# Three unused tiles of 32 bytes that shift where matmul operands start in SBUF

## The chip, the cores and the metric

The kernel runs on one core of one Trainium2 chip, as one launch. The metric is the time of the device in microseconds. Before the change it is 565.58 us, the median of three runs (565.38 to 565.63).

## The reference

Three layers follow each other, all in float32. The first is attention over hash buckets: two batches of 8 heads, 768 positions, 64 dimensions. The second is a feed-forward layer over the 1536 resulting rows of 512, with a softmax gate and a normalisation between its two products. The third sends each row to one of 8 experts of two products each.

```python
def _attn_ref(q, k, v, proj):
    q_bucket, k_bucket = ...                      # signs of q @ proj and k @ proj, as 6 bits
    scores = scale * np.matmul(q, k.transpose(0, 1, 3, 2))
    scores = np.where(q_bucket == k_bucket, scores, -1e9)
    attn = softmax(scores)
    return np.matmul(attn, v)

def _moe_ref(x, w_in, w_out, g_ln):               # 1536 x 512 -> 1024 -> 512
    h = x @ w_in
    solu = h * softmax(h)
    ln = (solu - mean(solu)) / np.sqrt(var(solu) + 1e-06) * g_ln
    return ln @ w_out

def _moe2_ref(x, w_gate, w_output_gate, w1, w2):  # 8 experts, 512 -> 1024 -> 512
    e_idx = np.argmax(x @ w_gate, axis=1)
    for e in range(8):
        mask = e_idx == e
        h = np.maximum(x[mask] @ w1[e], 0.0)
        out[mask] = gate_w[mask, None] * eom[mask, e, None] * (h @ w2[e])
```

## The kernel before

The order of every engine's work is written out by hand in the program; no scheduler moves anything. There are three stages.

**Attention** (class `Attention`, to about 207 us). The scores (line 243) are matmuls of 384 columns in pairs: the two heads of a pair lie on partitions 0 to 63 and 64 to 127, and each takes one half of TensorE's rows. Their operands are tiles `Hq`, `Lq`, `Fq`, `Hk`, `Lk`, `Fk` of type fp32r. The products with the values (line 294) and the sums (line 314) have plain float32 operands. During the first microseconds bf16 matmuls on a tile of zeros (`fill`, line 195) run, which compute nothing that is used; small bf16 products (`bits` with `tab`, line 228) make the bucket masks.

**Feed-forward** (class `Ffn`, about 211 to 367 us). For each of 12 blocks of 128 rows the first product (method `up`, line 634, tiles `h<-wi,xh` and `h<-wi,xl` in the profile) is two halves of 12 matmuls of 512 columns, and the second (method `down`, line 634, `y<-wo,lh` and `y<-wo,ll`, for some blocks `h<-wo,...`) is 24 matmuls of 512 columns. Each float32 operand is split into a high and a low part of type fp32r (`xh`, `xl`; `wi0`, `wi1`; `lh`, `ll`; `wo0`, `wo1`), and three of the four part products are added up in PSUM. In the profile's names the first tile behind the arrow is the moving operand, the second the stationary one (transposes the same: `t<-ident,e` moves the identity over the block `e`). Every matmul has a weight load of its own (PEld).

**Experts** (class `Experts`, about 375 to 559 us). Each of the 8 experts has 96 matmuls of 256 columns (line 1163: the rows `xh`, `xl` move, for expert 0 `e`; the weights `wh`, `wl` are stationary) and 48 of 512 columns (line 1185: the weights move, the halves of the hidden layer are stationary, which are kept in the tiles `wo0` and `wo1`, no longer needed as weights by then). Weights come by DMA into four staging tiles `ws` and are split into `wh` by ScalarE (line 1071) and `wl` by GpSimd and VectorE (line 1073) ahead of their use.

**Where the tiles lie.** A tile has one start address, the same in every partition. Tiles come from pools that lie one behind the other, from the left end of the SBUF or (with `side="right"`) from its right end; within a pool, tiles follow each other at multiples of 32 bytes. The first address and its remainder by 64, as the program is built before the change:

| tiles | start | remainder by 64 |
|---|---|---|
| attention: `Hk`, `Lk`, `Hq`, `Lq`, `Fk`, `Fq` | 81792 and on, every 3072 | 0 |
| attention: `pt0` to `pt7` in turn | 145024 and on, every 3104 | 0, 32, 0, 32, ... |
| zeros of the bf16 matmuls: `fill` | 52640 | 32 |
| `wi0`, `wi1` | 196576, 212960 | 32 |
| `wo0`, `wo1` | 19872, 36256 | 32 |
| feed-forward `xh`, `xl`, `lh`, `ll` | 97760 to 118240 | 32 |
| experts' `wh` and `wl` | 163808 and on, every 8192 | 32 |
| experts' `xh`, `xl`; `e`; `ws` | 116384; 85408; 52640 | 32 |
| `ident`, `ones`, `projw`, `wg32` | 17472, 17216, 17088, 16576 | 0 |

Inside a tile, the pieces that one matmul reads lie at multiples of 512 bytes, but for the query slices of the attention, which start 0, 4 or 8 bytes in.

Of the kernel before, what the change touches and what calls it, by code (L numbers as in the profile page):

```python
# [8 lines left out]
F32 = mybir.dt.float32  # L9
# [7 lines left out]
P = 128  # L17
# [1219 lines left out]
def counts(tc, C, cnt):  # L1237
    nc, ci = tc.nc, C["ci"]
    nc.vector.tensor_tensor(out=cnt, in0=cnt, in1=C["first"], op=ALU.subtract)
    nc.vector.tensor_reduce(out=C["gap"], in_=cnt, axis=AX.X, op=ALU.max)  # L1240
    nc.vector.tensor_copy(ci[:, 0:E], cnt)
    nc.vector.tensor_copy(ci[:, E:E + 1], C["gap"])
# [54 lines left out]
@with_exitstack  # L1297
def tile_kernel(
    ctx: ExitStack, tc, q, k, v, proj, moe_w_in, moe_w_out, moe_g_ln, moe2_w_gate, moe2_w_output_gate, moe2_w1, moe2_w2, out
):  # L1300
    nc = tc.nc
    cp = ctx.enter_context(tc.tile_pool(name="cp", bufs=1))
    scratch = tc.dram_tile([SLOTS + N, ROW], F32, name="scratch")
    cnt = cp.tile([P, E], F32, name="cnt")

    def clear(z, n):
        nc.sync.dma_start(
            out=scratch[4 * P * n:4 * P * (n + 1), :].rearrange("(p a) r -> p (a r)", p=P).rearrange("p (b x) -> p b x", b=10),
            in_=z.unsqueeze(1).to_broadcast([P, 10, 2 * ROW // 5]),
        )  # L1310

    def blank(z):
        nc.gpsimd.memset(z, 0.0)
        for n in range(3):
            nc.sync.dma_start(
                out=out[4 * P * n:4 * P * (n + 1), :].rearrange("(p a) r -> p a r", p=P),
                in_=z.unsqueeze(1).to_broadcast([P, 4, DM]),
            )

    with tc.manual_schedule(), ExitStack() as c0, ExitStack() as c4:  # L1320
        c1 = c0.enter_context(ExitStack())
        xp = c1.enter_context(tc.tile_pool(name="xT", bufs=1, side="right"))
        xT = xp.tile([P, 2, 4, S], F32, name="xT")
        keep = c4.enter_context(tc.tile_pool(name="wo", bufs=1))
        W = Weights(tc, cp, xp, keep, moe_w_in, moe_w_out, moe_g_ln, moe2_w_gate, moe2_w_output_gate)
        with ExitStack() as c2:
            cv = c2.enter_context(tc.tile_pool(name="cv", bufs=1))
            at = Attention(tc, c2, q, k, v, xT)
            at.load(0, "qk")
            at.C = C = {}  # L1330
            at.open(c2)
            make_consts(tc, cp, cv, proj, C)
            at.preset()
            nc.gpsimd.tensor_copy(cnt, C["first"])
            nc.gpsimd.memset(W.wg, 0.0)
            at.warm(10)
            at.tables()
            at.warm(1)
            z = cv.tile([P, 2 * ROW // 5], F32, name="zero")
            nc.gpsimd.memset(z, 0.0)  # L1340
            extra = W.steps(cv, at.bank)
            at.run(8, extra, [lambda n=n: clear(z, n) for n in range(7)])
        stg = c4.enter_context(tc.tile_pool(name="ws", bufs=4, reuse_waits="tile"))
        ep = c4.enter_context(tc.tile_pool(name="ep", bufs=2, reuse_waits="tile"))
        r0 = c4.enter_context(tc.tile_pool(name="r0", bufs=1, reuse_waits="tile"))
        ex = Experts(tc, C, stg, moe2_w1, moe2_w2, scratch, out, r0, W.wo)
        with ExitStack() as c2:
            ffn = Ffn(tc, c2, C, xT, W, scratch, cnt, ep, ex)
            for u in range(4):
                ex.fetch(u)  # L1350

            def ahead():
                c1.close()
                return ex.ahead(c0)

            ffn.run(ahead, blank)
        with ExitStack() as c2:
            ex.open(c2)
            ex.run(lambda: counts(tc, C, cnt))
    overflow(tc, C, moe2_w1, moe2_w2, scratch, out, ex.done)  # L1360
# [36 lines left out]
```

## Time and profile before

| what | us |
|---|---|
| median of three runs | 565.58 |
| the profiled execution, its own time | 566.14 |
| its span, first to last instruction | 564.4 |
| attention, to the last score matmul | about 207 |
| feed-forward products | 211 to 367 |
| experts' products | 375.5 to 558.5 |

The profiled execution lies 0.56 us above the median, and 1.7 us of its time lie outside the span. Engines are PE (TensorE's matmuls), PEld (its weight loads, which run beside matmuls), DVE (VectorE), ACT (ScalarE) and POOL (GpSimd). The duration of a matmul in the trace includes its way through the array, and matmuls overlap; how fast they follow each other is read from their starts. A row of the timeline merges equal instructions that follow each other on an engine, gives the start of the first, the time to the end of the last, and their number.

### The profile page before, as it was taken

The numbers are of one execution on the slowest core, as the hardware profiler recorded it, in microseconds if no ns is written. First come the engines' busy times: TensorE is split into PE (matmuls) and PEld (weight loads), VectorE is DVE, ScalarE is ACT, GpSimd is POOL, SyncE is SP. The second block draws the span as 40 slices with busy tenths as digits, with TensorE's granted clock in tenths as the row PEclk, the third lists the DMA queues.
The fourth block names the chain that finished last, engine by engine and source line by source line (L and its number), as shares of the span: only waits on it lengthen the run. The fifth ranks groups of instructions, "written<-read, shape, count | busy, mean of one in ns | idle before, by whom it ended". The sixth has DMA issues, their size and how long they took to land. (4 is left out here: it accounts for less than half of the span.)

```text
span 564.4 us, 9890 instructions
## 1 busy us (share of the span) xinstructions
PE 551.3 (98%) x3826; PEld 438.2 (78%) x3826; DVE 393.2 (70%) x793; ACT 266.1 (47%) x450; POOL 330.3 (59%) x270
## 2 busy tenths in 40 slices
PE   8899999999999999999999999999999999999995
PEld 3776667776667747888888887889989989899894
DVE  7978888888978657767687777665674664646631
ACT  3457657575675641332224232337355462564530
POOL 5399898898989883001001040327875956958741
PEclk9899999999999999999999999999999999999999
DMA  3545646455452445500000040329829376597201
GB/s 112 163 139 149 156 147 180 136 150 149 153 141 94 116 133 202 216 0 1 1 1 0 1 95 0 113 73 351 293 81 334 101 285 219 177 339 254 78 23 36
DMA packets 48100, 76.09 MB, mean 135 GB/s; under 512 B 11563, under 2 KB 20523, under 8 KB 48046
## 3 DMA queue, kind: packets, MB, share of 16 engines
q1 hardware_dynamic: 42910, 59.50, 33.2%
q10 hardware_dynamic: 2896, 9.57, 5.5%
q0 software_dynamic: 2240, 6.31, 3.3%
q8 instruction: 32, 0.52, 0.4%
q14 instruction: 22, 0.18, 0.1%
HBM read 58.39 MB, written 17.93 MB: 135 GB/s over the span
## 5 line engine op out<-in xcount | busy, mean ns | idle before, releaser
L1073 POOL TENSOR_TENSOR wl<-ws,wh 128x512 fp32r<-128x512 f32 x75 | 107.5, 1466 | 42.1 <-ACT wh L1071 42.1
L283 POOL TENSOR_TENSOR acc<-pt,pt 128x768 f32<-128x768 f32 x48 | 89.9, 1874 | 29.2 <-ACT pt L279 29.2
L255 DVE TENSOR_REDUCE m<-ps 128x2 f32<-128x768 f32 x96 | 87.9, 950 | 11.9 <-PE ps L243 9.5
L279 ACT ACTIVATE pt<-ps 128x768 f32<-128x768 f32 x96 | 76.4, 813 | 38.1 <-PE ps L243 38.0
L1185 PE MATMUL o<-wh,wo 128*128 128x512 f32 x256 | 82.6, 394 | 0.0
L1071 ACT CAST wh<-ws 128x512 fp32r<-128x512 f32 x128 | 70.5, 620 | 5.0 <-POOL wl L1073 2.4
L294 PE MATMUL ps<-pt,v 128*64 128x385 f32 x384 | 67.1, 493 | 0.0
L1073 DVE TENSOR_TENSOR wl<-ws,wh 128x512 fp32r<-128x512 f32 x53 | 58.1, 1129 | 11.7 <-ACT wh L1071 11.6
L616 POOL TENSOR_TENSOR xl<-xT,xh 128x512 fp32r<-128x512 f32 x12 | 15.4, 1288 | 86.4 <-ACT xh L625 56.3
L1169 DVE SCALAR_TENSOR_TENSOR wo<-g,wo 128x512 fp32r<-128x512 f32 x32 | 22.1, 691 | 53.2 <-ACT wo L1168 53.2
L285 POOL TENSOR_TENSOR acc<-acc 128x768 f32<-128x768 f32 x30 | 54.9, 1829 | 2.4
L1185 PEld LDWEIGHTS o<-wh,wo 128*128 128x128 f32 x256 | 48.1, 188 | 9.7
L1168 ACT ACTIVATE wo<-g 128x512 fp32r<-128x512 f32 x32 | 19.1, 598 | 75.7 <-PE g L1163 75.7
L294 PEld LDWEIGHTS ps<-pt,v 128*64 128x64 f32 x384 | 25.6, 136 | 34.3 <-issue 30.4
L1185 PE MATMUL o<-wl,wo 128*128 128x512 f32 x128 | 50.2, 392 | 0.0
L634 PE MATMUL h<-wi,xh 128*128 128x512 f32 x192 | 49.4, 399 | 0.0
L634 PE MATMUL y<-wo,lh 128*128 128x512 f32 x176 | 43.6, 398 | 0.0
L783 POOL DMA_INDIRECT scratch<-row,slot x12 | 11.8, 982 | 49.9 <-DVE cnt L810 22.9
L634 PEld LDWEIGHTS h<-wi,xh 128*128 128x128 f32 x192 | 34.9, 188 | 7.4 <-ACT xh L625 0.6
L634 PEld LDWEIGHTS y<-wo,lh 128*128 128x128 f32 x176 | 32.4, 188 | 7.8 <-issue 0.2
L243 PE MATMUL ps<-Hk,Hq 64*128 64x384 f32 x192 | 36.9, 375 | 1.1 <-DVE m L255 0.7
L243 PE MATMUL ps<-Hq,Hk 64*128 64x384 f32 x192 | 35.2, 363 | 1.0 <-DVE m L255 1.0
(228 smaller groups left out, 1139.2 us busy)
## 6 DMA issues: line engine op xcount, KB each, us to landing
ws<-in_moe_w_dram SPq DMA_DIRECT2D x32, 1024.0 KB, 8.4
scratch<-zero SPq DMA_DIRECT2D x7, 1030.0 KB, 6.9
r<-scratch SPq DMA_DIRECT2D x16, 257.5 KB, 2.7
raw<-in_moe_w_in_dram ACTq DMA_DIRECT2D x8, 512.0 KB, 4.4
raw<-in_moe_w_out_dram ACTq DMA_DIRECT2D x8, 512.0 KB, 3.7
v<-in_v_dram SPq DMA_DIRECT2D x8, 384.0 KB, 3.1
out_dram<-zero SPq DMA_DIRECT2D x3, 1024.0 KB, 6.6
q<-in_q_dram SPq DMA_DIRECT2D x7, 384.0 KB, 3.2
```

What stands on the lines that cost most here:

```text
L243: self.nc.tensor.matmul(ps[:, h], w[r], x[r], start=(n == 0), stop=(n == len(jobs) - 1), tile_position=(D * h, 0))
L255: nc.vector.tensor_reduce(out=st["m", i][:, c, :, kh], in_=ps, axis=AX.X, op=ALU.max, negate=True)
L279: nc.scalar.activation(out=pt[:, :, 0:HW], in_=ps, func=AF.Exp, scale=0.125)
L283: nc.gpsimd.tensor_tensor(out=acc, in0=st["pt", i, c - 1][:, :, 0:HW], in1=pt[:, :, 0:HW], op=ALU.add)
L285: nc.gpsimd.tensor_tensor(out=acc, in0=parts.pop(), in1=acc, op=ALU.add)
L294: nc.tensor.matmul(st["x", i][D * h:D * h + D, 0:HW + 1], st["v"][:, h, c, :], st["pt", i, c][:, h, 0:HW + 1], start=(c == 0), stop=(c == ...
L634: nc.tensor.matmul(ps, a[:, k, :], w[j](k), start=(n == 0), stop=(n == len(jobs) - 1))
L1071: nc.scalar.copy(hi[:, k, :], t[:, k, :])
L1073: eng.tensor_tensor(out=lo[:, k, :], in0=t[:, k, :], in1=hi[:, k, :].bitcast(F32), op=ALU.subtract)
L1168: nc.scalar.activation(out=hi, in_=ps, func=AF.Relu)
L1169: nc.vector.scalar_tensor_tensor(out=hl[:, 2 * g:2 * g + 2, :], in0=ps, scalar=0.0, in1=hi.bitcast(F32), op0=ALU.max, op1=ALU.subtract)
L1185: nc.tensor.matmul(st["o"][t], h[:, f, t * P:(t + 1) * P], w[:, f % 4, :], start=(f == 0 and n == 0), stop=(f == 7 and n == 2),)
```

## The change

Three tiles of 128 x 8 float32 (32 bytes in each partition) are allocated and never used. `edge` takes the right end of the SBUF, so that what lies at the right side (`xT`, `wi0`, `wi1`, later `wh`, `wl`) starts 32 bytes lower. `even` lies in the pool of constants, so that what lies to its right (`wo0`, `wo1`, staging, feed-forward, experts) starts 32 bytes higher. `odd` lies in the first pool of the attention, so that attention's own tiles start 64 bytes higher in all.

```diff
@@ tile_kernel
     cp = ctx.enter_context(tc.tile_pool(name="cp", bufs=1))
+    edge = ctx.enter_context(tc.tile_pool(name="edge", bufs=1, side="right"))
+    edge.tile([P, 8], F32, name="edge")
     scratch = tc.dram_tile([SLOTS + N, ROW], F32, name="scratch")
@@
         xT = xp.tile([P, 2, 4, S], F32, name="xT")
+        cp.tile([P, 8], F32, name="even")
         keep = c4.enter_context(tc.tile_pool(name="wo", bufs=1))
@@
             cv = c2.enter_context(tc.tile_pool(name="cv", bufs=1))
+            cv.tile([P, 8], F32, name="odd")
             at = Attention(tc, c2, q, k, v, xT)
```

No instruction is added, removed or moved: on each of the five engines the changed program has the same instructions, on the same tiles, in the same order and with the same waits. What differs are the addresses. After the change `wi0`, `wi1`, `wo0`, `wo1`, `xh`, `xl`, `lh`, `ll`, `wh`, `wl`, `e` and `ws` all start at a multiple of 64. The attention's operands `Hk` to `Fq` stay at multiples of 64 (81856 and on; they were at multiples of 128 and now lie 64 beside them), `pt0` to `pt7` alternate as before, `fill` stays at 32. `ident`, `ones`, `projw` and `wg32` go from 0 to 32. Small tiles of the routing go either way.

## Rows read from the trace of the kernel before

**Rows 1.** The page: engines' busy time, share of the span, instructions; granted clock

```profile
PE 551.3 (98%) x3826; PEld 438.2 (78%) x3826; DVE 393.2 (70%) x793; ACT 266.1 (47%) x450; POOL 330.3 (59%) x270
PEclk9899999999999999999999999999999999999999
```

**Rows 2.** Windows: length, then each engine's busy us, clock, DMA share, GB/s

```profile
211.00:367.00 156.00, 155.32 (x847) 127.44 (x846) 113.34 (x367) 47.91 (x92) 25.41 (x32) 1.00 0.18 59
375.50:558.50 183.00, 182.53 (x1210) 165.64 (x1208) 103.73 (x141) 88.39 (x164) 124.42 (x107) 1.00 0.58 200
...
382.00:406.00 24.00, 24.00 (x162) 21.87 (x161) 14.88 (x20) 13.69 (x26) 20.50 (x18) 1.00 0.95 323
```

**Rows 3.** Waits of PE from 211 us on: us, times, longest

```profile
PE t L697 <- DVE e L684: 0.7, 1, 0.7
...
PE g L1163 <- DVE e L1099: 0.5, 1, 0.5
PE t L1029 <- DVE oh L811: 0.3, 1, 0.3
```

**Rows 4.** Whole span, matmuls alone of lines 634, 1163, 1185, 243 in turn

```profile
0.00:564.40 564.40, 139.51 (x576) 1.00 0.43 135
...
0.00:564.40 564.40, 89.56 (x768) 1.00 0.43 135
...
0.00:564.40 564.40, 91.14 (x384) 1.00 0.43 135
...
0.00:564.40 564.40, 113.91 (x1152) 1.00 0.43 135
```

**Rows 5.** Timeline of PE, first and third of three bf16 matmuls: start, us

```profile
4.26 0.38 PE L195 MATMUL ps<-fill 128*128 128x512 bf16 x1
...
4.69 0.38 PE L195 MATMUL ps<-fill 128*128 128x512 bf16 x1
```

**Rows 6.** Timeline of PE, feed-forward's first product

```profile
213.91 1.98 PE L634 MATMUL h<-wi,xh 128*128 128x512 f32 x8
215.73 1.07 PE L634 MATMUL h<-wi,xl 128*128 128x512 f32 x4
216.63 1.98 PE L634 MATMUL h<-wi,xh 128*128 128x512 f32 x8
```

**Rows 7.** Timeline of PE, feed-forward's second product

```profile
266.55 3.89 PE L634 MATMUL y<-wo,lh 128*128 128x512 f32 x16
270.29 2.03 PE L634 MATMUL y<-wo,ll 128*128 128x512 f32 x8
272.15 0.39 PE L634 MATMUL h<-wi,xh 128*128 128x512 f32 x1
```

**Rows 8.** Timeline of PE, expert 2: first product, from its first row to the second

```profile
426.86 0.62 PE L1163 MATMUL g<-xh,wh 128*128 128x256 f32 x4
...
433.66 0.39 PE L1185 MATMUL o<-wh,wo 128*128 128x512 f32 x1
...
440.29 0.40 PE L1185 MATMUL o<-wh,wo 128*128 128x512 f32 x1
```

**Rows 9.** Timeline of PE, expert 0, first product

```profile
379.02 1.10 PE L1163 MATMUL g<-e,wh 128*128 128x256 f32 x8
379.96 0.64 PE L1163 MATMUL g<-e,wl 128*128 128x256 f32 x4
380.43 1.10 PE L1163 MATMUL g<-e,wh 128*128 128x256 f32 x8
```

**Rows 10.** Timeline of PE, transposes

```profile
262.47 0.60 PE L724 MATMUL t<-ident,row 128*128 128x128 f32 x4
262.91 0.93 PE L697 MATMUL t<-ident,e 128*128 128x128 f32 x7
```

**Rows 11.** Timeline of PE, attention: the first and ninth of nine fp32r pairs, bf16 pairs

```profile
100.44 0.34 PE L243 MATMUL ps<-Hq,Hk 64*128 64x384 f32 x2
...
101.86 0.34 PE L243 MATMUL ps<-Hq,Hk 64*128 64x384 f32 x2
...
67.80 0.50 PE L228 MATMUL ps<-bits,tab 64*128 64x384 bf16 x4
```

**Rows 12.** Lines 228 and 279: duration ns min/median/max

```profile
L228 PE MATMUL ps<-bits,tab x32: 319/323/333, 7.6 to 165.5; 64*128 64x384 bf16 x32
...
L279 ACT ACTIVATE pt<-ps x96: 799/813/817, 19.4 to 206.7; 128x768 f32<-128x768 f32 x96
```

## The prediction

> **What bounds the kernel now.** I read the page's busy times first: PE is busy for 551.3 of 564.4 us, and the granted clock is 9 of 10 in all slices but one [rows 1]. A table by stage shows the same where the change acts: 155.3 of 156 us in the feed-forward stage, 182.5 of 183 in the experts', at a granted clock of 1.00, and the next engine there is DVE with 113 of 156 and POOL with 124 of 183 [rows 2]. The waits of PE from 211 us on are three, 1.5 us in all [rows 3]. So the end is set by how fast matmuls follow each other, and since no instruction moves, the change can only act through the pace of single instructions. A busy PE says nothing of that pace, so the third view is the timeline, where a start minus the start before it is one matmul's share.
>
> The best pace on record for 512 columns is that of the bf16 matmuls on zeros: two steps from 4.26 to 4.69, 0.215 us each [rows 5]; 512 columns at 2.4 GHz, the higher level of the clock, would be 0.213. The fp32r matmuls of the same size are slower, at the same clock. Feed-forward, first product: 12 matmuls from 213.91 to 216.63, 226.7 ns each [rows 6]. Second product: 24 from 266.55 to 272.15, 233.3 ns each [rows 7]. Experts' second product: the first and the 30th matmul start at 433.66 and 440.29, so 29 steps in 6.63 us, 228.6 ns each [rows 8]. Experts' first product, 256 columns: 60 from 426.86 to 433.66, 113.3 ns each [rows 8], half of 226.7; and for expert 0, whose rows lie in another tile, 12 from 379.02 to 380.43, 117.5 ns each [rows 9].
>
> The number to look at is 226.7 = 2 x 113.3: the loss goes with the columns, not with the matmul. Against 213.3 and 106.7 ns it is one part in sixteen, and sixteen float32 columns are 64 bytes. All these moving operands start 32 bytes beside a multiple of 64. That is the pattern of a read of 64 bytes that straddles a border each time and pays one cycle of 17 for it. bf16, with half the bytes per column, lies at 32 too and doesn't pay, which fits a read that has slack.
>
> **The change part by part.** *The aligned operands.* If the straddle is the cause, 512 columns fall to the bf16 pace of 215 ns, and 256 columns to what a weight load allows: the transposes, 128 columns each with a load of its own, follow at 0.44 / 4 = 0.11 us, 109 to 110 ns [rows 10]; I take 109. The counts are 576 matmuls in line 634, half of them of each product, 768 in line 1163 and 384 in line 1185 [rows 4]. The part of each that is above 226.7 (233.3 in one product, 228.6 in another, 117.5 against 113.3) differs between operands that all lie at 32, so I do not lay it to the 32 bytes, and keep it:
> - feed-forward, first product: 288 x (226.7 - 215) = 3.4 us
> - feed-forward, second product: 288 x 11.7 = 3.4 us, keeping 6.6 ns of each
> - experts' second product: 384 x 11.7 = 4.5 us, keeping 1.9 ns
> - experts' first product: 768 x (113.3 - 109) = 3.3 us
>
> That is 14.6 us. All of it is on the path, since PE waits for nobody there. If what I keep goes as well, add 288 x 6.6 + 384 x 1.9 + 96 x 4.2 ns = 1.9 + 0.7 + 0.4 = 3.0 us: 17.6 us, the far end on this side. The near end is nothing, and below it the third rival. I take 14.6.
>
> *Attention.* Its operands were at multiples of 64 and stay so. The fp32r pairs take 1.42 / 8 = 177.5 ns [rows 11], and bf16 pairs of the same shape 0.50 less one duration of 0.323, about 177 ns [rows 11, 12]. So with aligned operands fp32r is as slow as bf16 and no slower, whatever a pair costs beside its 160 ns of columns; that speaks for the straddle, though a pair that has another limit could hide it. I cost its move from multiples of 128 to multiples of 64 at nothing, because that is a placement at 64 as well; should each of 1152 / 2 = 576 pairs [rows 4] pay the same part in sixteen, 10 ns, it is 5.8 us.
>
> *Tiles that go from 0 to 32* (`ident`, `ones`, `projw`). Transposes are held by the weight load, their moving operand has only 128 columns, and the float32 products run in two passes at half the pace of columns. I cost them at nothing; one part in sixteen of 109 ns for some 220 transposes would be 1.5 us.
>
> *Other engines.* ScalarE writes `pt0` to `pt7`, which lie at 0 and 32 in turn, in 799 to 817 ns [rows 12]: so 32 or 64 is worth at most 2% to it, and it is not on the path.
>
> *A page on the other side.* The rows above show a loss of one part in sixteen and cannot say which border it comes from. The Trainium skill, "SBUF — State Buffer", section "Door 1: The DMA port swizzle", says that SBUF lines are 16 bytes and that each crossing to a new line costs. By that rule 32 and 64 are alike, each being a multiple of 16, and the sum would be 0 us. No run here shows the size of a line.
>
> **The sum.** The profiled execution took 566.1 us in itself, 564.4 in its span. The terms are differences of steps in it, and they are 2.6% of it, so they carry over to the median of 565.6 as they are: 565.6 - 14.6 = 551.0 us.
>
> **The rivals.** *No change: the part in sixteen belongs to fp32r.* Then 17 cycles for 16 columns is what four bytes a column cost at the full clock, wherever they start, and every pace above stays. For it: first and second product differ though both are at 32, so other causes than the 32 bytes exist; and 384 columns x 17/16 at 2.4 GHz are 170 ns, which with a few ns between the halves of a pair is near the 177.5 of the aligned pairs. Against it: bf16 pairs take as long. Time 565.6.
>
> *The gain is made in part and eaten in part.* The chain of the softmax in the feed-forward stage (DVE 113 of 156 us) or the arrival of the weights for the first experts (DMA share 0.95 from 382 to 406) becomes late [rows 2]. PE waits 1.5 us in all now [rows 3], so some slack is there but none of the views says how much. If the whole share of the feed-forward stage were lost, 6.8 us: 551.0 + 6.8 = 557.8.
>
> *Slower: the distance between operands counts, not their start.* The two sides move in opposite directions, so the distance from `wi` to `xh`, from the experts' `xh` to `wh` and from `wh` to `wo` changes by 64 bytes, while that from `wo` to `lh` stays. Moving operand and weight load read at the same time, and the paces 226.7 and 233.3, 113.3 and 117.5 show that two placements at 32 can differ by 3 to 4%. If the good placements become like the bad: 288 x 6.6 + 672 x 4.2 + 384 x 4.7 ns = 1.9 + 2.8 + 1.8 = 6.5 us, 572.1; with half of them, 568.9. It decides if the first product's 226.7 rises toward 233 while the second product's stays. For it: that difference is in the trace, and alignment cannot explain it. Against it: only the extra above 226.7 is at stake, and as many placements could get better.
>
> **How the numbers follow.** The forecast has 0.52, since one explanation fits 226.7, 113.3, bf16 and the pairs; no change 0.21; part of the gain 0.10; slower 0.17. A difference under 0.2%, 1.1 us, can't be told from none here. Faster holds the first and the third: 0.62. The forecast's own range is 546.5 (all 17.6 us and 1.5 us of transposes' and waits' side effects) to 555. The range for 8 in 10 reaches to no change and a little over: 546.5 to 567.0; most of the slower case is left out.
>
> **What would show it.** Right: 12 matmuls of the first product in 2.58 to 2.61 us in place of 2.72, 60 of 256 columns in 6.55 in place of 6.80, the same clock, attention's length unchanged, PE still at 98%. The step of the kept extra is wrong if the second product falls to 215 too. Wrong altogether: 226.7 and 113.3 stand. The slower rival shows as 226.7 rising while the second product's 233.3 stays; the eaten gain as new waits of PE for DVE or ACT at a faster pace.

## The result and the profile after

The changed kernel takes 570.92 us (median of 4 runs, 570.52 to 571.18) where the kernel before, beside it, takes 565.48 (4 runs, 565.16 to 565.63): a ratio of 1.0098 [1.0083, 1.0112]. It is 5.4 us slower. I had forecast 551.0 us and a range that ends at 567.0.

The profiled execution took 571.15 us, its span 569.4, which is 5.0 more than before. The page, as [rows 1], is first: TensorE is still the bound, busy 98% of the span at the full clock, and the 5 us stand in its own busy time (551.3 before).

```profile
PE 556.3 (98%) x3826; PEld 442.6 (78%) x3826; DVE 394.2 (69%) x793; ACT 266.0 (47%) x450; POOL 330.8 (58%) x270
PEclk9899999999999999999999999999999999999999
```

The table by stage, in the same columns and over the same two stretches as [rows 2]:

```profile
211.00:367.00 156.00, 155.39 (x842) 126.58 (x841) 112.34 (x354) 47.74 (x91) 25.53 (x32) 1.00 0.17 57
375.50:558.50 183.00, 182.53 (x1193) 166.94 (x1192) 103.89 (x141) 88.76 (x164) 123.94 (x105) 1.00 0.57 198
```

PE is as busy as before in both stretches, at the same clock of 1.00, but it gets through 842 matmuls in the first where it was 847, and 1193 in the second where it was 1210. So each matmul takes longer. It is not waiting: its waits from 211 us on are the same three as in [rows 3].

```profile
PE t L697 <- DVE e L684: 0.6, 1, 0.6
PE g L1163 <- DVE e L1099: 0.5, 1, 0.5
PE t L1029 <- DVE oh L811: 0.3, 1, 0.3
```

Which matmuls, the busy time by line tells: the whole span, lines 634, 1163, 1185 and 243 in turn, as [rows 4].

```profile
0.00:569.40 569.40, 140.73 (x576) 1.00 0.42 134
...
0.00:569.40 569.40, 93.99 (x768) 1.00 0.42 134
...
0.00:569.40 569.40, 90.57 (x384) 1.00 0.42 134
...
0.00:569.40 569.40, 113.88 (x1152) 1.00 0.42 134
```

Against [rows 4] the feed-forward's line has 1.22 us more, the experts' first product 4.43 more, the experts' second product 0.57 less and attention 0.03 less. That is +5.05 us, the whole difference of the spans.

The timeline gives the paces. Feed-forward, both products, and the transposes, as [rows 6], [rows 7] and [rows 10]; then expert 0 and expert 2, as [rows 9] and [rows 8]:

```profile
213.98 2.03 PE L634 MATMUL h<-wi,xh 128*128 128x512 f32 x8
215.85 1.10 PE L634 MATMUL h<-wi,xl 128*128 128x512 f32 x4
216.78 2.03 PE L634 MATMUL h<-wi,xh 128*128 128x512 f32 x8
...
263.08 0.60 PE L724 MATMUL t<-ident,row 128*128 128x128 f32 x4
263.51 1.04 PE L697 MATMUL t<-ident,e 128*128 128x128 f32 x8
...
267.22 3.90 PE L634 MATMUL y<-wo,lh 128*128 128x512 f32 x16
270.95 2.03 PE L634 MATMUL y<-wo,ll 128*128 128x512 f32 x8
272.82 2.03 PE L634 MATMUL h<-wi,xh 128*128 128x512 f32 x8
...
380.17 1.12 PE L1163 MATMUL g<-e,wh 128*128 128x256 f32 x8
381.13 0.64 PE L1163 MATMUL g<-e,wl 128*128 128x256 f32 x4
381.61 1.12 PE L1163 MATMUL g<-e,wh 128*128 128x256 f32 x8
...
428.75 0.64 PE L1163 MATMUL g<-xh,wh 128*128 128x256 f32 x4
...
435.95 0.40 PE L1185 MATMUL o<-wh,wo 128*128 128x512 f32 x1
...
440.28 0.39 PE L1185 MATMUL o<-wl,wo 128*128 128x512 f32 x1
...
441.64 0.39 PE L1185 MATMUL o<-wl,wo 128*128 128x512 f32 x1
```

- Feed-forward, first product: 12 matmuls in 2.80 us, 233.3 ns each; it was 226.7.
- Second product: 24 in 5.60 us, 233.3 ns; unchanged.
- Experts' first product: 60 from 428.75 to 435.95, 120.0 ns; it was 113.3. Expert 0: 12 in 1.44 us, 120.0; it was 117.5.
- Experts' second product: 6 from 440.28 to 441.64, 226.7 ns; it was 228.6.
- Transposes: 0.43 us for 4, where it was 0.44.

The second product is the one whose two operands moved the same way. That it stands while the first rises is the mark that the prediction gave for its rival "the distance between operands counts". In this table, worked out from the programs' layouts, a distance is the start of the moving operand less that of the stationary one, modulo 256 bytes:

| product (moving, stationary) | distance before | after | ns before | ns after |
|---|---|---|---|---|
| feed-forward first (`wi`, `xh`) | 0 | 192 | 226.7 | 233.3 |
| feed-forward second (`wo`, `lh`) | 192 | 192 | 233.3 | 233.3 |
| experts' first (`xh`, `wh`), 256 columns | 192 | 0 | 113.3 | 120.0 |
| the same for expert 0 (`e`, `wh`) | 192 | 0 | 117.5 | 120.0 |
| experts' second (`wh`, `wo`) | 64 | 0 | 228.6 | 226.7 |

### The profile page after: what moved, and what is told of

The parts are those of the page before. It is cut to its first block, busy times and chain, and to the rows that moved or that the text cites. A ratio compares the mean times of both kernels' runs of the same rounds, so it can differ in the third digit from the quotient of the medians.

```text
span 569.4 us, 9890 instructions
## 1 busy us (share of the span) xinstructions
PE 556.3 (98%) x3826; PEld 442.6 (78%) x3826; DVE 394.2 (69%) x793; ACT 266.0 (47%) x450; POOL 330.8 (58%) x270
```

## The experiments

Each time is compared with the kernel before, run beside it on the same chip.

**1. Aligned, at the old distances.** All the operands that the change aligns lie at multiples of 64, but their distances are those of before, modulo 256 (and 512).

```diff
+    edge = ctx.enter_context(tc.tile_pool(name="edge", bufs=1, side="right"))
+    edge.tile([P, 8], F32, name="edge")
@@
+        cp.tile([P, 120], F32, name="even")
@@
+            cv.tile([P, 8], F32, name="odd")
```

> Operands of feed-forward and experts start at multiples of 64 as in the changed kernel, but both sides are moved by the same amount (right side 32 bytes down, left side 480 up, which is 32 down modulo 512), so every distance between a moving operand and a stationary one is that of the kernel before, modulo 512. Theory distance: paces of before, 226.7 ns in the first feed-forward product, 113.3 ns in the experts' first, time 565.5 +- 0.8 us. Theory start (a start at a multiple of 64 is what makes reads slower): paces of the changed kernel, 233.3 and 120 ns, time 571 +- 0.8 us.

565.15 us (10 runs), ratio 0.9999 [0.999, 1.0009]. The busy times of lines 634, 1163 and 1185, to be read beside [rows 4]:

```profile
0.00:572.00 572.00, 139.50 (x576) 1.00 0.42 133
...
0.00:572.00 572.00, 89.53 (x768) 1.00 0.42 133
...
0.00:572.00 572.00, 91.16 (x384) 1.00 0.42 133
```

Before they were 139.51, 89.56 and 91.14. Whether the operands start at a multiple of 64 or 32 beside one is worth nothing here, and the forecast's cause falls.

**2. The distances alone.** One pad of 64 bytes on the left; every operand stays 32 bytes beside a multiple of 64, and the distances are those of after.

```diff
+        cp.tile([P, 16], F32, name="even")
```

> All operands stay 32 bytes beside a multiple of 64 as before, but the left side is moved by 64 bytes against the right, which is the change of distance that the changed kernel has. Theory distance: 233.3 ns in the first feed-forward product, 120 ns in the experts' first, 226.7 in the experts' second, time 571 +- 0.8 us. Theory start: paces of before, 226.7, 113.3 and 229 ns, time 565.5 +- 0.8 us.

570.89 us, ratio 1.0101 [1.0084, 1.0118]. The same three lines, which after had 140.73, 93.99 and 90.57:

```profile
0.00:572.00 572.00, 140.76 (x576) 1.00 0.42 133
...
0.00:572.00 572.00, 94.00 (x768) 1.00 0.42 133
...
0.00:572.00 572.00, 90.58 (x384) 1.00 0.42 133
```

The result of the change comes back without its alignment. Experiments 1 and 2 together show that the distance between the operands is the whole cause.

**3. A map of distances.** fp32r matmuls on PE alone, 24 for each pair of starts; `STAT` is (0, 1).

```diff
+        for cols in (512, 256):
+            for b in STAT:
+                for a in range(16):
+                    for _ in range(24):
+                        nc.tensor.matmul(
+                            ps[:, 0:cols], st[:, 8 * b:8 * b + P], mv[:, 8 * a:8 * a + cols], start=True, stop=True
+                        )
```

> Leaves out the whole computation (writes zeros) and measures pace by itself: runs of 24 fp32r matmuls with one stationary and one moving operand, of 512 columns and of 256, the moving operand's start going through 16 multiples of 32 bytes, for a stationary operand at 0 and at 32 modulo 512. Theory distance: the pace is the same for equal distance at both stationary starts; 512 columns: 226.7 ns at distance 0, 233.3 at 64 below, 229 at 64 above; 256 columns: 113.3 at 192 above, 120 at 256. Theory start: the pace goes by the moving start alone, 226.7 and 113.3 where it is 32 beside a multiple of 64 and 233.3 and 120 at multiples of 64. The forecast's own reason (a straddled read) would have 215 and 109 at multiples of 64.

Blocks of the timeline of PE, each asked for by itself (a row begins with the last matmul of the block before it): 512 columns at distance 32, at 0 (starts 256 and 0), at 0 again (starts 32 and 32), then 256 columns at distance 192 and at 0.

```profile
12.04 5.52 PE L69 MATMUL ps<-mv,st 128*128 128x512 f32 x23
...
51.16 5.41 PE L69 MATMUL ps<-mv,st 128*128 128x512 f32 x23
...
101.36 5.41 PE L69 MATMUL ps<-mv,st 128*128 128x512 f32 x23
...
202.02 2.79 PE L69 MATMUL ps<-mv,st 128*128 128x256 f32 x23
...
233.06 2.91 PE L69 MATMUL ps<-mv,st 128*128 128x256 f32 x23
```

A row less one duration (0.39 us, or 0.28) over its steps is the pace with the way into it: 5.13 / 22 = 233 ns at distance 32, 5.02 / 22 = 228 at both places of distance 0. The settled paces, the mean of the last steps of each block, hang in this map on the distance alone:

| distance | 0 | 32 | 64 | 96 | 128 | 160 | 192 | 224 |
|---|---|---|---|---|---|---|---|---|
| 512 columns, ns | 226.7 | 233.3 | 228.8 | 233.3 | 233.3 | 234.3 | 233.3 | 233.3 |
| 256 columns, ns | 120.0 | 117.8 | 117.8 | 120.0 | 118.8 | 117.5 | 113.3 | 118.0 |

The four products of both kernels stand in it: 0, 192 and 64 for 512 columns, 192 and 0 for 256. The best distance for 512 columns is the worst for 256. Nothing is faster than 226.7 and 113.3 at any start.

**4. One distance undone.** The changed kernel with 192 bytes ahead of the experts' `xh`, so that their first product is back at 192.

```diff
+        pool("xpad", 1).tile([P, 48], F32, name="xpad")
         self.xp = pool("xe", 2)
```

> The changed kernel with 192 unused bytes ahead of the experts' xh and xl, which gives the experts' first product of experts 1 to 7 back its distance of before (moving 192 above stationary, modulo 256), its starts staying at multiples of 64. Theory distance: that product goes back from 120.0 to 113.3 ns, 672 x 6.6 ns = 4.4 us, and the time from 570.9 to 566.5 +- 0.8 us, the first feed-forward product staying at 233.3. Theory start: 120 ns and 571 us stay.

569.24 us, ratio 1.0072 [1.0057, 1.0088]: better than after, by far less than expected (line 1163 has 92.55 us, where after had 93.99). Expert 2's first product in the timeline:

```profile
426.88 0.64 PE L1164 MATMUL g<-xh,wh 128*128 128x256 f32 x4
...
435.36 0.39 PE L1186 MATMUL o<-wh,wo 128*128 128x512 f32 x1
```

72 matmuls in 8.48 us, 117.8 ns, neither 120.0 nor 113.3. The distance is that of before and the pace is not. Something else takes part.

**5. Distance 0 for `wo`.** The kernel before with pads on both sides of the pool of `wo`: the feed-forward's and the experts' second products go to distance 0, the first products stay.

```diff
+        cp.tile([P, 16], F32, name="pad64")
         keep = c4.enter_context(tc.tile_pool(name="wo", bufs=1))
         W = Weights(...)
+        keep.tile([P, 48], F32, name="pad192")
```

> The kernel before, with wo0 and wo1 moved by 64 bytes (all that lies to their right by 256, nothing modulo 256), so that the feed-forward's second product and the experts' second have distance 0 modulo 256, as the feed-forward's first has. Theory distance: the feed-forward's second product falls from 233.3 to 226.7 ns (288 x 6.6 = 1.9 us), the experts' second from 229 to 226.7 (384 x 2.2 = 0.8 us), the time from 565.3 to 562.6 +- 0.7 us, faster than both kernels. Theory start: all operands are 32 beside a multiple of 64 as before, so 565.3 stays.

566.08 us (11 runs), ratio 1.0018 [1.0009, 1.0027]; expected was a gain. The three lines:

```profile
0.00:572.00 572.00, 137.97 (x576) 1.00 0.42 133
...
0.00:572.00 572.00, 92.00 (x768) 1.00 0.42 133
...
0.00:572.00 572.00, 90.27 (x384) 1.00 0.42 133
```

Lines 634 and 1185 gain 1.5 and 0.9 us against [rows 4], as meant. Line 1163, whose operands kept their distance, loses 2.4: experts 1 to 7 go at 117.8 ns, as in experiment 4. In both kernels the matmuls ahead of it go at 226.7. The three lines cancel, so the 0.9 us that this kernel is slower are not in them; its trace has one wait of PE more than before, 0.3 us for a DMA (`t<-ident,r`, line 1020), and the rest is not accounted for.

**6. Shorter loads, and bf16.** Another map, on PE alone: bf16, fp32r with 64 and 32 stationary columns, and fp32r pairs of 64 rows.

```diff
+        for a in range(8):
+            for _ in range(24):
+                nc.tensor.matmul(ps[:, 0], bs[:, 0:P], bm[:, 16 * a:16 * a + 512], start=True, stop=True)
+        for rows in (64, 32):
+            for a in range(8):
+                for _ in range(24):
+                    nc.tensor.matmul(ps[0:rows, 0], st[:, 0:rows], mv[:, 8 * a:8 * a + 512], start=True, stop=True)
... the same for the pairs of 64 rows
```

> Leaves out the whole computation (writes zeros) and measures pace by itself, for 8 distances modulo 256 each: bf16 operands of 512 columns with 128 stationary columns; fp32r operands of 512 columns with 64 and with 32 stationary columns; fp32r pairs of 384 columns on half the rows each, as the attention's, with stationary columns side by side and at every third place. If moving reads and weight loads get in each other's way: bf16 stays at 215.8 at all distances, and 226.7 of fp32r falls toward 215.8 as the weight load gets shorter; the pairs vary with distance by some 5 ns or more. If one part in sixteen is the price of fp32r columns by themselves: 226.7 stays with 64 and 32 stationary columns at the best distance, and only what is above it shrinks.

bf16 in the timeline, over 10 us of it:

```profile
19.78 10.52 PE L71 MATMUL ps<-bm,bs 128*128 128x512 bf16 x48
```

Less one duration of 0.38, 10.14 / 47 = 215.7 ns; the settled pace is 215.8 at all eight distances. fp32r with 64 stationary columns (loads of 134 ns in the trace) is best at 160 (226.7) and 228.3 to 231.7 elsewhere; with 32 columns (108 ns), 230.0 to 240.0. So a shorter load did not bring fp32r below 226.7, and the best distance shifts with the length of the load. The pairs of 64 rows take 173.3 to 176.7 ns with the stationary columns side by side, and 176.7 to 178.7 with every third. Of what was expected if reads and loads get in each other's way, only the part on bf16 came true: 226.7 did not fall, and the pairs vary by 3.4 and 2.0 ns, not by 5. The rival's mark, 226.7 at the best distance, held with 64 columns and not with 32.

**7. Distance 0 for the second product alone.** The kernel before with 192 bytes ahead of `lh` and `ll`; the experts lie where they lay.

```diff
+        pool("lpad", 1).tile([P, 48], F32, name="lpad")
         self.lp = pool("lp", 2)
```

> The kernel before with 192 unused bytes between the feed-forward's xh, xl and its lh, ll, and nothing else moved that a product of the experts or the attention reads. The feed-forward's second product gets distance 0 modulo 256. Theory distance with entry: it falls from 233.3 to about 227.5 ns, 288 x 5.8 = 1.7 us, and since the experts' second product keeps its distance of 64, their first is entered as before and keeps 113.3: 563.5 +- 0.6 us, faster than both kernels. If the distance of one stage cannot be chosen without loss in the next: 565.2.

564.26 us (11 runs) beside 565.46, ratio 0.9981 [0.9972, 0.999]. It beats the kernel before by 1.2 us, a little less than the 1.7 that were expected. The three lines, the second product, and expert 0's first product in the timeline:

```profile
0.00:572.00 572.00, 138.18 (x576) 1.00 0.41 133
...
0.00:572.00 572.00, 89.15 (x768) 1.00 0.41 133
...
0.00:572.00 572.00, 91.06 (x384) 1.00 0.41 133
```

```profile
265.28 3.80 PE L635 MATMUL y<-wo,lh 128*128 128x512 f32 x16
268.92 1.98 PE L635 MATMUL y<-wo,ll 128*128 128x512 f32 x8
270.73 2.01 PE L635 MATMUL h<-wi,xh 128*128 128x512 f32 x8
...
377.16 1.07 PE L1164 MATMUL g<-e,wh 128*128 128x256 f32 x8
...
378.52 1.07 PE L1164 MATMUL g<-e,wh 128*128 128x256 f32 x8
```

24 matmuls in 5.45 us, 227.1 ns, where it was 233.3 [rows 7]. The experts' first product keeps its fast pace, 89.15 us against 89.56. What it has less is expert 0's: 12 matmuls in 1.36 us, 113.3 ns, where [rows 9] has 117.5, though its operands lie where they lay.

**8. What the pace ahead does.** Blocks of 24 matmuls of 512 columns, each followed by 48 of 256, at chosen distances.

```diff
+        for a, b in ((0, 0), (2, 6), (0, 6), (6, 6), (4, 6), (2, 6), (0, 6), (2, 0), (0, 0)):
+            for _ in range(24):
+                nc.tensor.matmul(ps, st[:, 0:P], mv[:, 8 * a:8 * a + 512], start=True, stop=True)
+            for _ in range(48):
+                nc.tensor.matmul(ps[:, 0:256], st[:, 0:P], mv[:, 8 * b:8 * b + 256], start=True, stop=True)
```

> Leaves out the whole computation (writes zeros): 24 fp32r matmuls of 512 columns at one distance, and right behind them 48 of 256 columns at another, for nine pairs of distances. Theory entry: 256 columns at distance 192 keep 113.3 ns behind 512 columns at distance 64, and 117.7 behind 512 columns at distance 0, each time it is tried; at distance 0 they take 120 behind both. Rival (256 columns have one pace for each distance, and something else in the real kernel made 117.7): 113.3 behind both.

Blocks two, three and six of the timeline: distances 64 then 192, 0 then 192, and 64 then 192 again.

```profile
17.56 5.77 PE L67 MATMUL ps<-mv,st 128*128 128x512 f32 x24
23.16 5.61 PE L69 MATMUL ps<-mv,st 128*128 128x256 f32 x48
28.61 5.62 PE L67 MATMUL ps<-mv,st 128*128 128x512 f32 x24
34.07 5.82 PE L69 MATMUL ps<-mv,st 128*128 128x256 f32 x48
...
61.81 5.67 PE L67 MATMUL ps<-mv,st 128*128 128x512 f32 x24
67.32 5.81 PE L69 MATMUL ps<-mv,st 128*128 128x256 f32 x48
```

256 columns at distance 192 take 5.61 us behind the first of these, and 5.82 and 5.81 behind the others: settled, 113.3 ns against 117.7, for the same two addresses. 512 columns at distance 64 also have two paces, 233.4 (17.56) and 228.8 (61.81). Over all nine pairs, distance 192 took the fast rhythm behind each of three blocks at 233.3 or 233.4 and the slow one behind each of three at 226.7 or 228.8, and distance 0 took 120.0 all three times. So half of the expectation failed: behind distance 64 it was once the fast one and once the slow one. "One pace per distance" is wrong: some distances hold two rhythms, and what runs ahead makes the difference. The pace ahead is not the rule, though. In the kernel before, experts 2 to 7 take 113.3 behind second products that settle at 228.9, and behind 228.8 this test took 117.7. That kernel also has both rhythms at distance 192: 117.5 for expert 0 [rows 9] and 113.3 for the others [rows 8]. Which step of the entry decides is open.

**9. The left side alone.** `even` and `odd` without `edge`: distances change by 32 bytes and not by 64.

```diff
+        cp.tile([P, 8], F32, name="even")
@@
+            cv.tile([P, 8], F32, name="odd")
```

> Two of the three tiles alone (even and odd): the left side moves up by 32 bytes and starts at multiples of 64, the right side stays 32 beside. Theory distance: all distances between the sides shrink by 32, which by the map is 233.3 in place of 226.7 ns in the feed-forward's first product, about 118 in place of 113.3 in the experts' first, 233.3 in place of 229 in the experts' second: 288 x 4 + 672 x 4.5 + 384 x 4.3 ns = 1.2 + 3.0 + 1.7 = 5.9 us, 571 +- 1 us. Theory start: half of the operands aligned, half of the changed kernel's loss, 568.

571.47 us, ratio 1.011 [1.0095, 1.0126], as expected from the map. The three lines:

```profile
0.00:572.00 572.00, 140.61 (x576) 1.00 0.42 133
...
0.00:572.00 572.00, 92.79 (x768) 1.00 0.42 133
...
0.00:572.00 572.00, 92.57 (x384) 1.00 0.42 133
```

Another split than after's, for a sum not far from it (+5.8 against +5.1 us in these three lines): line 1185 has 1.43 us more than before, where after had 0.57 less, and line 1163 has 3.23 more, where after had 4.43. So the map works for a layout that it was not read from.

## Why the prediction was wrong

**The step that failed** is "If the straddle is the cause, 512 columns fall to the bf16 pace". The part in sixteen above 213.3 and 106.7 ns was laid to starts 32 bytes beside a multiple of 64. Experiment 1 moved the starts and nothing changed; the map has no start with less than 226.7; shorter loads do not lower it either. The rival "the part in sixteen belongs to fp32r" had this right: bf16 takes 215.8 in the same place. The support from the attention was a little off besides: 0.50 less one duration [rows 11, 12] goes from the first matmul to the fourth, the second half of the next pair. By the starts of the first and the third, 67.80 and 67.97, a bf16 pair takes 0.17 us (173 ns before rounding), so the fp32r pairs at 177.5 were slower by 4 ns. All four terms of the 14.6 us rest on this step, so all four are nothing.

**What I set aside was what moved.** I kept "the part of each that is above 226.7" as not belonging to the 32 bytes and gave it 3.0 us at the far end of a gain. That part is the effect of distance (for expert 0's 117.5, of the rhythm), and the change alters three of four distances. The evidence was in the rows: two products with the same 32 bytes and different paces [rows 6, 7]. An explanation of 226.7 that could not explain 233.3 had 0.52, the rival that explained it 0.17, and the range left it out.

**The slower rival** had place and mark right, 568.9 to 572.1 against 570.9, but that its time fits is in part luck, since two of its terms are too large and one is too small:
- Feed-forward, first product: 1.9 us; line 634 has 1.22 more. The 226.7 of [rows 6] is the settled pace. By the starts of all its matmuls the mean before was about 229, since most runs of it take 2 to 9 steps to settle (one goes 231, 236, 228, 233, 230 ns), and after it is 233.3 from the outset.
- Experts' first product: 2.8 us; line 1163 has 4.43 more. I took expert 0's 117.5 [rows 9] as the pace of a bad placement, but its distance is that of the other experts (the second rhythm of experiment 8), and the worst is 120.0, which distance 0 brings.
- Experts' second product: 1.8 us more; it is 0.57 less. Distance 64 to 0 is a gain at 512 columns. The rival could say that placements change, not which way; the map says it.

**What held.** PE is the bound and what its pace loses reaches the end in full: lines +5.05, span +5.0. The clock, the waits and the other engines are as before. Attention, moved by 64 bytes as a whole, so that the distances in it stay, costs 113.88 against 113.91. Transposes cost nothing more.

**The page on the other side.** Experiment 1 shows starts at 32 and at 64 alike. By the 16-byte lines of the Trainium skill ("SBUF — State Buffer", section "Door 1: The DMA port swizzle") these starts are alike too, so there the run agrees, with its ratio of 0.9999; the rule does not contain the distance that cost the 5 us.

**The mechanism** is shown as far as this: at fixed columns the pace hangs on where the moving read lies against the stationary read, it shifts when the load gets shorter, bf16 is free of it, and some distances hold two rhythms. Matmul reads and weight loads that get in each other's way in SBUF would give a pace that goes by their distance, but experiment 6 did not bear out what that account said of shorter loads and of pairs, so it is argued and not shown. The Trainium skill ("TensorE: Matmul & The Clock Gate", section "Step-by-step: what each phase is for") gives TensorE two independent read ports, so that a load of the next weights takes no bandwidth from the running matmul. For bf16 the map agrees, 215.8 at every distance; for fp32r, 226.7 to 234.3 by distance alone, it does not. What in the memory has a period of 256 bytes no run here shows, nor why fp32r has its floor at 17/16.

## What to carry to other kernels

When a stream of equal instructions runs at two paces in one trace, compare how its operands lie to each other before their alignment, and explain the spread before spending the common part. A pad in one pool moves the distances of every later stage, so move one product's operand alone, and read the pace of each stage again, since behind a stage that is made faster the next can fall into a worse rhythm (experiment 5: 2.4 us won in two lines, 2.4 us lost in the third). Take a settled pace for a rate only after counting how many steps the stage needs to settle.

## What the runs showed of the hardware

- An fp32r matmul's pace, behind a weight load of its own, depends on the distance of its two operands modulo 256 bytes: 226.7 to 234.3 ns for 512 columns, 113.3 to 120.0 for 256, with opposite preferences at 0.
- At equal distances, starts at multiples of 64 and starts 32 beside them gave the same time (ratio 0.9999 [0.999, 1.0009]).
- bf16 shows none of it: 215.8 ns at eight distances.
- One distance can hold two rhythms for the same two addresses (113.3 and 117.7; 228.8 and 233.4), and what runs ahead makes the difference; by which of its properties is open.
